# Longer PE warm-up, full-height contraction and a shared reciprocal in an attention and two-layer-MLP kernel

## The chip, the cores and the metric

The kernel runs on one core of one Trainium2 chip. The metric is the device time of one execution in microseconds (us). Five engines work side by side, each through its own queue in order: PE (TensorE, matrix products, with its weight loads shown as PEld), DVE (VectorE), ACT (ScalarE), POOL (GpSimd) and SP (SyncE, which here issues every DMA).

## The reference, cut to what matters

```python
scores = q @ k.T / sqrt(64)                     # 4 batches x 8 heads, 576 rows, 64 wide
decay  = cum[:, None] - cum[None, :]            # cum = cumsum(log(clip(f, 1e-4, 1)))
scores = where(causal, -1e9, scores + decay)
attn   = exp(scores - rowmax); attn /= rowsum + 1e-9
x      = attn @ v                               # 2304 tokens x 512
h = relu(x @ w_in); x = (h * h) @ w_out                        # 512 -> 2048 -> 512
h = x @ w_in2; y = where(h >= 1, h, where(h <= -1, 0, (h+1)**2 / 4)); out = y @ w_out2
```

## The kernel before, in words

The tokens are split into five blocks of up to 512. A block goes through the two MLPs as 32 steps (16 slices of 128 hidden units for each layer): `h_group` (L1006, products of L1016: x times w_in, 12 products of 512 columns for a full block), `act_group` (the nonlinearity) and `out_group` (L1054, products of L1067 to L1069 into accumulators). Every operand is split in a high and a low half and multiplied as three products. Weights come in as 64-bit floats, are decoded on ACT, DVE and POOL (L925 to L958), split (L976), stored to a scratch array in DRAM and read back by later blocks.

Attention of the first 256 query rows of each head (`HEAD`) is done by `attention32` (L591), in groups of four heads (`QUAD`). Groups 0 to 3 make up block 0, and stand ahead of everything else; groups 4 to 7 belong to block 1 and are interleaved with the MLP steps of block 0. The other rows are done by `attention` (L699) during later steps.

For each head of a group, `attention32` does in turn: the scores (L640, two fp32 products, of 128 and of 256 columns; the trace has two records for each product), a masked row maximum on DVE (L587), exp with row sums on ACT (L647), sum + 1e-9 and reciprocal on DVE (L652, L653, operation `o_r`), a scaling of E by the reciprocal on ACT, DVE or POOL (L661 to L663), three transposes on PE (L669) and a copy out of PSUM. After each second head, four products with v (L683) give the head pair's output, which is copied to `x` (L693, L695).

The score product gets the decay through extra rows of its contraction. `QK[0]` and `QK[1]` are two buffers of 128 partitions that groups take in turn. Rows 0 to 63 hold k and q. Rows 64 and 65 hold, on the K side, cum and the constant 8, and on the Q side the constant -8 and cum. `clear` (L546 to L554) sets rows 64 and 65 of both buffers to 8 and -8 with four memsets each (L555 in the trace: buffer 0 on DVE, buffer 1 on POOL). DMAs then write cum over one of the two rows on each side: for group 0 straight from the scan's result (`first_rows`, L507, once all memsets of buffer 0 are done), and for later groups from a copy in DRAM (L616). The score products use rows 0 to 65 (`kr`, `qr`: `reg()[:D + 2, ...]`).

`setup` (L474) loads f, clips it (L488, DVE), takes its logarithm (L490, ACT), scans it (L491, DVE), and stores cum (L503). Zeroing of the constant buffers Q2 and K2 (L517, L518) shares DVE and POOL with it. `warm_up` (L534) issues `WARM` = 11 products of the identity with itself on PE (L542) before the first scores.

The order on each engine is written at build time by a planner (`Schedule`, L152). Every operation has a due time, a cost and its dependences; of the operations that can start, the planner takes the one that is due first, tries several weights, and emits the shortest plan's order. On the chip each engine follows this order and waits on semaphores.

Of the kernel before, what the change touches and what calls it, by code (L numbers as in the profile page):

```python
# [8 lines left out]
F32 = mybir.dt.float32  # L9
# [7 lines left out]
AF = mybir.ActivationFunctionType  # L17
ALU = mybir.AluOpType

B, H, S, D = 4, 8, 576, 64  # L20
DM, DFF = 512, 2048
NT = B * S
P = 128
# [7 lines left out]
HEAD = 256  # L31
REST = S - HEAD
CHUNKS = [(HEAD, 320), (320, 448), (448, S)]
# [14 lines left out]
QUAD = 4  # L48
SPARE = ("E", "g", "E", "o", "E", "r", "E", "g", "E", "o")

SLAV = [0.0, 0.51, 0.75, 0.75, 0.0]
# [2 lines left out]
VE = [5.5, 6.1]  # L54
RE = [1.36, 7.73, 16.0]
LW = 29.1
WARM = 11


def pattern(bits):  # L60
# [320 lines left out]
def tile_attention_moe_moe(ctx: ExitStack, tc: tile.TileContext, qkv, f, w2, outT):  # L381
    nc = tc.nc
    PSUM = bass.MemoryType.PSUM
    W64 = w2.dtype == U64
    sch = Schedule()
# [4 lines left out]
    def ring(tag, n, shape, dt, space=None, fifo=True, most=()):  # L390
        kw = {"space": space} if space else {}
        tp = ctx.enter_context(tc.tile_pool(name="p_" + tag, bufs=n, **kw))
        pools[tag] = (Pool(n, fifo, most), tp, shape, dt)

    def new(tag, name, shape=None, dt=None, kind=None):
        p, tp, sh, d = pools[tag]
        shape = sh if shape is None else shape
        kw = {"padded_shape": sh} if list(shape) != list(sh) and len(shape) == len(sh) and dt is None else {}
        return Buf(p, lambda: tp.tile(shape, dt or d, tag=tag, name=name, **kw), kind)
# [3 lines left out]
    ring("K1", 2, [P, S], F32R)  # L403
    ring("vt", 3, [P, 5, 2, 64], F32R)
    ring("E", 5, [P, S], F32)
    ring("st", 4, [P, 3, len(CHUNKS)], F32)
    ring("mm", 3, [P, 2], F32)
    ring("PP", 3, [P, (2 * NK - 1) * P], F16)
    ring("PT", 2, [P, QUAD * 4 * HEAD], F16)
# [31 lines left out]
    for s in range(NS):  # L441
        g, att = s // NFC, 0.0
# [29 lines left out]
    QK = [new("PT", f"QK{i}", [P, QUAD * 2 * HEAD], F32) for i in range(2)]  # L472
# [75 lines left out]
    def clear(i, half):  # L548

        n = QUAD * HEAD  # L550
        rows = lambda a, z: QK[i].tile[a:z, n * half:n * half + n]
        kq = lambda a, z, t: rows(a, z).rearrange("p (c t n) -> p c t n", t=2, n=HEAD)[:, :, t, :]
        due = -98 + 2 * i + half
        eng, m = ("POOL", nc.gpsimd) if i else ("DVE", nc.vector)  # L554
        fill = lambda out, x: {eng: (n / 1920 + 0.03, lambda: m.memset(out(), x))}  # L555
        return [sch.op(due, fill(lambda t=t, x=x: kq(D, D + 2, t), x), [], [QK[i]]) for t, x in ((0, 8.0), (1, -8.0))]

    cleared = {(i, half): clear(i, half) for i in range(2) for half in range(2)}

# [4 lines left out]
    def copies(out, in_, n, engines="ACT DVE POOL", psum=False):  # L564

        alts = {}
        if "ACT" in engines:
            alts["ACT"] = (act_t(n, psum), lambda: nc.scalar.activation(out(), in_(), AF.Copy))  # L568
        if "DVE" in engines:
            alts["DVE"] = (  # L570
                dve_t(n) if psum else dve2_t(n), lambda: nc.vector.tensor_copy(out(), in_()), *([] if psum else [True]))  # L571
        if "POOL" in engines:
            alts["POOL"] = (pool_t(n), lambda: nc.gpsimd.tensor_scalar(  # L573
                out(), in_(), 1.0, 0.0, op0=ALU.mult, op1=ALU.add))
        return alts
# [15 lines left out]
    def attention32(g):  # L591

        first = g.blk == 0
        qk, n = QK[g.i % 2], QUAD * 2 * HEAD
        reg = lambda: qk.tile
        kr = lambda c: reg()[:D + 2, 2 * c * HEAD:2 * c * HEAD + HEAD]
        qr = lambda c: reg()[:D + 2, 2 * c * HEAD + HEAD:2 * c * HEAD + 2 * HEAD]
        wait = groups[g.i - 2].qk if g.i >= 2 else ()
        src = qkv[g.at:g.at + D * n].rearrange("(p n) -> p n", p=D)
        loads, parts = [], 2 if g.i == 0 else 1  # L600
# [25 lines left out]
            in_=qkv[g.at_v:g.at_v + P * vn].rearrange("(p n) -> p n", p=P)))}, [], [vt], early=VE[g.i] if g.i < len(VE) else g.due - 4)  # L626
        g.qk = []
        chunks = [(0, 0, P), (1, P, HEAD)]
        for c in range(QUAD):
            nm = f"{g.i}q{c}"  # L630
            t0 = g.due + g.len * c / QUAD
            a = c % 2
            Eb = new(SPARE[len(used) % len(SPARE)] if first else "E", f"E{nm}", [P, 3 * P])
            used.append(Eb)
            st = new("st", f"st{nm}")
            ps = new("acc" if first else "ps", f"s{nm}", kind="att")
            cols = lambda ci: slice(0, P) if ci == 0 else slice(P, 3 * P)
            o_e = []
            for ci, qa, e in chunks:
                o_s = sch.op(t0, {"PE": (4 * e / 2400, lambda c=c, ci=ci, qa=qa, e=e, ps=ps: nc.tensor.matmul(  # L640
                    ps.tile[:, cols(ci)], qr(c)[:, qa:qa + P], kr(c)[:, :e], start=True, stop=True))},
                    ready[c], [ps, Eb, qk])
                g.qk.append(o_s)
                o_t = sch.op(t0 + 0.3, {"DVE": (dve_t(e) + 0.01, lambda ci=ci, qa=qa, e=e, Eb=Eb, ps=ps, st=st: top(
                    Eb.tile[:, cols(ci)], ps.tile[:, cols(ci)], qa, e, P, -0.125, st.tile[:, 0, ci:ci + 1]))},
                    [o_s, mask_op[0]], [ps, Eb, st])
                o_e.append(sch.op(t0 + 0.8, {"ACT": (act_t(e, ptr=1) + 0.09, lambda ci=ci, Eb=Eb, st=st: nc.scalar.activation(  # L647
                    Eb.tile[:, cols(ci)], Eb.tile[:, cols(ci)], AF.Exp, scale=-1.0, bias=st.tile[:, 0, ci:ci + 1],
                    accum_out=st.tile[:, 1, ci:ci + 1]))}, [o_t], [Eb, st]))

            def recip(st=st):
                nc.vector.tensor_scalar(st.tile[:, 1, :2], st.tile[:, 1, :2], 1e-9, None, op0=ALU.add)  # L652
                nc.vector.reciprocal(st.tile[:, 2, :2], st.tile[:, 1, :2])  # L653

            o_r = sch.op(t0 + 2, {"DVE": (0.30, recip, True)}, o_e, [st])
            o_n = []
            for ci, qa, e in chunks:
                x = lambda ci=ci, Eb=Eb: Eb.tile[:, cols(ci)]
                r = lambda ci=ci, st=st: st.tile[:, 2, ci:ci + 1]
                o_n.append(sch.op(t0 + 2.5, {  # L660
                    "ACT": (act_t(e, ptr=1), lambda x=x, r=r: nc.scalar.activation(x(), x(), AF.Copy, scale=r())),  # L661
                    "DVE": (dve2_t(e), lambda x=x, r=r: nc.vector.tensor_scalar(x(), x(), r(), None, op0=ALU.mult), True),
                    "POOL": (pool_t(e), lambda x=x, r=r: nc.gpsimd.tensor_scalar(  # L663
                        x(), x(), r(), 0.0, op0=ALU.mult, op1=ALU.add)),
                }, [o_r], [Eb, st]))
            if a == 0:
                pr = new("pr", f"pr{nm}")
            tr = new("acc" if first else "ps", f"tr{nm}", kind="att")
            got = [sch.op(t0 + 3, {"PE": (0.11, lambda tr=tr, Eb=Eb, to=to, at=at: nc.tensor.transpose(  # L669
                tr.tile[:, to:to + P], Eb.tile[:, at:at + P], ident))}, [o_n[at > 0], id_op], [Eb, tr, pr])  # L670
                for to, at in ((0, 0), (P, P), (2 * P, 2 * P))]
            o_c = sch.op(t0 + 3.5, copies(
                lambda pr=pr, a=a: pr.tile[:, a, :3 * P].bitcast(F32), lambda tr=tr: tr.tile[:, :3 * P], 3 * P,
                "ACT DVE", psum=True), got, [tr, pr])
            if a == 0:
                o_c0 = o_c
                continue
            av = new("acc" if first else "ps", f"av{nm}", kind="att")
            o_m = None
            for kc in range(HEAD // P):  # L680
                def mms(c=c, kc=kc, pr=pr, av=av):
                    for i in range(2):
                        nc.tensor.matmul(  # L683
                            av.tile[D * i:D * i + D, kc * P:HEAD], v32(c - 1 + i, kc),
                            pr.tile[:, i, 2 * P * kc:2 * P * kc + HEAD - kc * P].bitcast(F32),
                            start=(kc == 0), stop=(kc == HEAD // P - 1))

                o_m = sch.op(t0 + 4, {"PE": (4 * (HEAD - kc * P) / 2400 + 0.05, mms)},
                             [o_c, o_c0, o_v, o_m], [av, vt, pr], SLAV[g.blk])
            x = xb[g.blk]  # L690
            kc = (g.h + c) // 2
            hi = lambda kc=kc: x.tile[:, kc, 0, g.off:g.off + HEAD]
            o3 = sch.op(t0 + 5, copies(hi, lambda av=av: av.tile[:, :HEAD], HEAD, "ACT DVE", psum=True), [o_m], [av, x])  # L693
            xops.setdefault((g.blk, kc), []).append(sch.op(t0 + 5.5, {
                "DVE": (dve_t(HEAD), lambda kc=kc, hi=hi, av=av: nc.vector.tensor_tensor(  # L695
                    x.tile[:, kc, 1, g.off:g.off + HEAD], av.tile[:, :HEAD], hi().bitcast(F32), op=ALU.subtract))},
                [o3], [av, x]))

    def attention(t):  # L699
        g, W, nm, due = t.b * H + t.h, REST, t.name, t.due  # L700
# [80 lines left out]

        def recip():
            nc.vector.tensor_scalar(
                st.tile[:, 1, :], st.tile[:, 1, :], 1e-9, unit, op0=ALU.add, op1=ALU.mult)
            nc.vector.reciprocal(st.tile[:, 2, :], st.tile[:, 1, :])  # L785

        o_r = sch.op(back(9.5), {"DVE": (0.30, recip, True)}, o_e, [st])

        o_t = []
# [409 lines left out]
```

## Time and profile before

| | us |
|---|---|
| median of 3 runs | 958.58 (956.57 to 959.28) |
| the profiled execution, its own time | 955.24 |
| its span in the profile | 953.5 |
| PE busy | 939.9 (99%) |
| DVE, ACT, POOL busy | 583.2, 638.0, 191.3 |

The span runs from the first to the last instruction of the profile. The granted clock (PEclk) is a share of TensorE's full 2.4 GHz: 1.00 is 2.4 GHz and 0.50 is 1.2 GHz. PE's busy time is modelled: its products are pipelined and their records overlap, so it tells that PE had work, not that it ran at its peak. "Share" of DMA is the mean busy share of the 16 DMA engines.

### The profile page before, as it was taken

The page shows a single profiled execution, that of the slowest core. Times are in us where ns is not written, and L with a number is a line of the kernel's source. Part 1 is how long each engine was busy: PE and PEld are TensorE (multiplying, and loading weights), DVE is VectorE, ACT ScalarE, POOL GpSimd, SP SyncE. Part 2 cuts the span into 40 slices and gives each one's busy share as a digit, 9 for nine tenths or more (in the row PEclk, how much of TensorE's full clock was granted, in tenths as well). Part 3 has the DMA queues.
Part 4 walks back from the last instruction along what each step waited for, and adds up shares of the span by engine and source line. Part 5 has one row for each costly group of instructions (what it writes and reads, how often), then busy time and mean ns, then how long its engine had stood idle before and what let it go on. Part 6 is the DMA issues. An engine that isn't in the chain of part 4 may idle for free.

```text
span 953.5 us, 14248 instructions
## 1 busy us (share of the span) xinstructions
PE 939.9 (99%) x4758; PEld 789.2 (83%) x4758; DVE 583.2 (61%) x1325; ACT 638.0 (67%) x1269; POOL 191.3 (20%) x341
## 2 busy tenths in 40 slices
PE   8999999999999999999999999999999999999998
PEld 6777777777778888888888888788888888889998
DVE  6899999989757668777767667866311132220032
ACT  5999879997877768787777677686432343334454
POOL 3321010134122323342323124231000000002200
PEclk6999999999999999999999999999999999999999
DMA  6699998996998987898899988796665655659994
GB/s 192 207 337 402 339 403 292 369 347 227 349 321 246 277 247 251 231 285 248 242 257 287 253 261 238 208 300 186 248 232 178 202 194 181 207 189 374 365 374 143
DMA packets 126106, 254.73 MB, mean 267 GB/s; under 512 B 89808, under 2 KB 90480, under 8 KB 104080
## 3 DMA queue, kind: packets, MB, share of 16 engines
q1 hardware_dynamic: 126032, 253.81, 81.0%
q8 instruction: 38, 0.62, 0.3%
q14 instruction: 36, 0.29, 0.1%
HBM read 194.35 MB, written 38.45 MB: 244 GB/s over the span
## 4 chain that ended last, share of the span: by engine, by line
PE 90%; DVE 4%; DMA 4%; issue 1%; ACT 1%; SPq 0%; POOL 0%; DVEq 0%; ACTq 0%
PE h L1016 39%; PE acc L1067 13%; PE acc L1069 13%; PE acc L1068 13%; PE av L840 4%; PE s L761 2%; PE s L762 2%; DMA PT<-PP 2%; DMA in<-in_qkv_dram 1%; DMA out_dram<-o 1%; PE s1q L640 1%; DVE whl L993 0%; DVE wf L957 0%; PE s0q L640 0%; DVE low L942 0%
## 5 line engine op out<-in xcount | busy, mean ns | idle before, releaser
L1016 PE MATMUL h<-x,whl 128*128 128x512 f32 (+1 forms) x1896 | 432.5, 371 | 0.6 <-DVE whl L993 0.5
L1016 PEld LDWEIGHTS h<-x,whl 128*128 128x128 f32 x1896 | 325.7, 189 | 55.4 <-issue 2.1
L1067 PE MATMUL acc<-gh,whl 128*128 128x512 f32 (+1 forms) x640 | 240.1, 375 | 2.9 <-DVE o L571 2.9
L1069 PE MATMUL acc<-gl,whl 128*128 128x512 f32 (+1 forms) x640 | 237.2, 371 | 0.0
L1068 PE MATMUL acc<-gh,whl 128*128 128x512 f32 (+1 forms) x640 | 236.7, 370 | 0.0
L580 DVE TENSOR_TENSOR gl<-g,gh 128x512 fp32r<-128x512 f32 (+1 forms) x126 | 83.6, 663 | 120.1 <-PE acc L1069 81.5
L1069 PEld LDWEIGHTS acc<-gl,whl 128*128 128x128 f32 x640 | 121.0, 189 | 21.5 <-POOL gl L582 0.2
L1067 PEld LDWEIGHTS acc<-gh,whl 128*128 128x128 f32 x640 | 120.9, 189 | 20.9 <-DVE o L571 3.4
L1068 PEld LDWEIGHTS acc<-gh,whl 128*128 128x128 f32 x640 | 121.0, 189 | 15.7
L1034 ACT ACTIVATE r<-h 128x512 f32<-128x512 f32 (+1 forms) x80 | 44.0, 550 | 91.3 <-PE h L1016 82.6
L1047 DVE SCALAR_TENSOR_TENSOR g<-r,h 128x512 f32<-128x512 f32 (+1 forms) x80 | 50.4, 630 | 80.1 <-ACT r L1045 79.6
L582 POOL TENSOR_TENSOR gl<-g,gh 128x512 fp32r<-128x512 f32 (+1 forms) x34 | 39.7, 1169 | 287.3 <-PE acc L1069 213.6
L1043 ACT ACTIVATE r<-h,half 128x512 f32<-128x512 f32 (+1 forms) x80 | 51.1, 639 | 61.9 <-PE h L1016 61.6
L815 DVE SCALAR_TENSOR_TENSOR PP<-E,st,PP 128x512 f16<-128x512 f32 (+2 forms) x128 | 77.6, 638 | 11.0 <-ACT PP L811 10.1
L778 ACT ACTIVATE E<-E,st 64x320 f32<-64x320 f32 (+2 forms) x96 | 63.6, 662 | 24.1 <-DVE st L587 15.6
L587 DVE CUSTOM_DVE_ANT_0 E<-s,mask 128x288 f32<-128x288 f32 (+2 forms) x128 | 62.1, 502 | 28.3 <-PE s L762 20.1
L811 ACT ACTIVATE PP<-E,st 128x512 f16<-128x512 f32 (+2 forms) x128 | 68.9, 591 | 9.1 <-DVE st L785 7.7
L840 PEld LDWEIGHTS av<-pr,vt 128*128 128x128 f32 x288 | 53.9, 189 | 13.0 <-issue 1.7
L840 PE MATMUL av<-pr,vt 128*128 128x320 f32 (+2 forms) x288 | 61.8, 287 | 1.3 <-DVE pr L571 1.3
L568 ACT ACTIVATE gh<-g 128x512 fp32r<-128x512 f32 (+1 forms) x70 | 40.7, 581 | 31.5 <-DVE g L1047 31.1
L573 POOL TENSOR_SCALAR pr<-PT 128x640 fp32r<-128x640 f16 (+2 forms) x50 | 31.2, 627 | 108.4 <-PE av L840 57.3
L568 ACT ACTIVATE pr<-PT 128x640 fp32r<-128x640 f16 (+2 forms) x63 | 36.3, 580 | 18.2 <-DMA PT<-PP 11.8
(258 smaller groups left out, 1145.4 us busy)
## 6 DMA issues: line engine op xcount, KB each, us to landing
whl<-scr SPq DMA_DIRECT2D x112, 1024.0 KB
raw<-in_w_dram SPq DMA_DIRECT2D x28, 1024.0 KB
scr<-whl SPq DMA_DIRECT2D x28, 1024.0 KB
in<-in_qkv_dram SPq DMA_DIRECT2D x32, 608.0 KB
whl<-scr SPq DMA_DIRECT2D x32, 512.0 KB
out_dram<-o SPq DMA_DIRECT2D x16, 256.0 KB
QK<-in_qkv_dram SPq DMA_DIRECT2D x7, 512.0 KB
raw<-in_w_dram SPq DMA_DIRECT2D x6, 512.0 KB
```

Source lines behind the costliest of these rows:

```text
L568: alts["ACT"] = (act_t(n, psum), lambda: nc.scalar.activation(out(), in_(), AF.Copy))
L580: alts["DVE"] = (dve_t(n), lambda: nc.vector.tensor_sub(out(), a(), b()), True)
L587: return nc.vector.tensor_tensor_reduce(out=out, in0=ps, in1=mask[:m, OFF - q0:OFF - q0 + n], scale=scale, scalar=3e38, op0=ALU.add, op1=A ...
L778: nc.scalar.activation(Ec.tile[:m, :e], Ec.tile[:m, :e], AF.Exp, scale=-1.0, bias=nmx(), accum_out=st.tile[:m, 1, ci:ci + 1])))}, [*tops, ...
L811: nc.scalar.activation(hi, x, AF.Copy, scale=r())
L815: nc.vector.scalar_tensor_tensor(lo, x, r(), hi, op0=ALU.mult, op1=ALU.subtract)
L840: nc.tensor.matmul(av.tile[:, c0:W], vt.tile[:, kc, :, :], pr.tile[:, i, :n], start=(kc == 0 and i == 0), stop=(kc == NK - 1))
L1016: nc.tensor.matmul(ps.tile[:, :n], w.tile[:, 0, wi, kc * P:(kc + 1) * P], src.tile[:, kc, xi, :n], start=(kc == 0 and i == 0), stop=(kc == ...
L1043: o1 = sch.op(due, {"ACT": (act_t(n, True, 1), lambda: A.activation(r.tile[:, :n], ps(), AF.Relu, scale=0.5, bias=half))}, [o], [psb, r])
L1067: nc.tensor.matmul(a.tile[:, :n], wh, gh.tile[:, :n], start=(fc == 0), stop=False)
L1068: nc.tensor.matmul(a.tile[:, :n], wl, gh.tile[:, :n], start=False, stop=False)
L1069: nc.tensor.matmul(a.tile[:, :n], wh, gl.tile[:, :n], start=False, stop=(fc == NFC - 1))
```

## The change

`WARM` goes from 11 to 17. The score products contract over all 128 rows of `QK` instead of 66; for this `clear` fills rows 64 to 127 with 8 on the K side and 0 on the Q side, and then row 64 of the Q side with -8 (three memsets instead of two for each half buffer). From group 1 on, two heads share one `st` tile, and with it one addition and one reciprocal over four columns, which wait for the exps of both heads; group 0 keeps one for each head. `attention32` is cut for this into `exps`, `recips`, `probabilities` and `products`. The `st` tile has four columns instead of three, and `attention` uses three of them.

```diff
-WARM = 11
+WARM = 17
...
-    ring("st", 4, [P, 3, len(CHUNKS)], F32)
+    ring("st", 4, [P, 3, 4], F32)
...
-        return [sch.op(due, fill(lambda t=t, x=x: kq(D, D + 2, t), x), [], [QK[i]]) for t, x in ((0, 8.0), (1, -8.0))]
+        kr = sch.op(due, fill(lambda: kq(D, P, 0), 8.0), [], [QK[i]])
+        qr = sch.op(due, fill(lambda: kq(D, P, 1), 0.0), [], [QK[i]])
+        return [kr, sch.op(due, fill(lambda: kq(D, D + 1, 1), -8.0), [qr], [QK[i]])]
...
-        kr = lambda c: reg()[:D + 2, 2 * c * HEAD:2 * c * HEAD + HEAD]
-        qr = lambda c: reg()[:D + 2, 2 * c * HEAD + HEAD:2 * c * HEAD + 2 * HEAD]
+        kr = lambda c: reg()[:, 2 * c * HEAD:2 * c * HEAD + HEAD]
+        qr = lambda c: reg()[:, 2 * c * HEAD + HEAD:2 * c * HEAD + 2 * HEAD]
...
-            def recip(st=st):
-                nc.vector.tensor_scalar(st.tile[:, 1, :2], st.tile[:, 1, :2], 1e-9, None, op0=ALU.add)
-                nc.vector.reciprocal(st.tile[:, 2, :2], st.tile[:, 1, :2])
-
-            o_r = sch.op(t0 + 2, {"DVE": (0.30, recip, True)}, o_e, [st])
+        def recips(c, st, n, deps):
+            def recip():
+                nc.vector.tensor_scalar(st.tile[:, 1, :n], st.tile[:, 1, :n], 1e-9, None, op0=ALU.add)
+                nc.vector.reciprocal(st.tile[:, 2, :n], st.tile[:, 1, :n])
+
+            return sch.op(g.due + g.len * c / QUAD + 2, {"DVE": (0.30, recip, True)}, deps, [st])
...
+        for c in range(0, QUAD, 2):
+            got = []
+            if g.i == 0:
+                for a in range(2):
+                    st = new("st", f"st{g.i}q{c + a}")
+                    Eb, o_e = exps(c + a, st, 0)
+                    got.append(probabilities(c + a, st, 0, Eb, recips(c + a, st, 2, o_e)))
+            else:
+                st = new("st", f"st{g.i}q{c}")
+                (E0, o0), (E1, o1) = (exps(c + a, st, 2 * a) for a in range(2))
+                o_r = recips(c + 1, st, 4, [*o0, *o1])
+                got = [probabilities(c + a, st, 2 * a, Eb, o_r) for a, Eb in enumerate((E0, E1))]
+            products(c + 1, got)
```

## Rows read from the trace of the kernel before

**Rows 1.** The page: the span, and part 1, busy time by engine.

```profile
span 953.5 us, 14248 instructions
...
PE 939.9 (99%) x4758; PEld 789.2 (83%) x4758; DVE 583.2 (61%) x1325; ACT 638.0 (67%) x1269; POOL 191.3 (20%) x341
```

**Rows 2.** Windows: length, busy (count) PE, PEld, DVE, ACT, POOL, clock, DMA, GB/s.

```profile
5.33:8.74 3.41, 0.65 (x6) 0.45 (x4) 2.81 (x7) 1.66 (x4) 1.54 (x5) 1.00 0.60 163
8.74:25.81 17.07, 16.73 (x59) 12.68 (x61) 9.54 (x53) 9.72 (x36) 1.68 (x4) 0.50 0.66 202
25.81:45.16 19.35, 19.07 (x138) 13.93 (x134) 17.53 (x84) 18.04 (x57) 6.66 (x14) 1.00 0.74 220
45.16:100.00 54.84, 54.84 (x258) 43.70 (x259) 52.97 (x98) 53.08 (x97) 11.71 (x5) 1.00 0.97 365
100.00:250.00 150.00, 149.32 (x697) 117.64 (x696) 140.01 (x246) 130.31 (x212) 27.50 (x30) 1.00 0.90 332
...
264.74:268.15 3.41, 3.41 (x10) 2.85 (x11) 1.72 (x6) 2.80 (x7) 0.00 (x0) 0.50 1.09 329
```

**Rows 3.** Line L542 (warm-up) in two stretches: duration in ns, min/median/max.

```profile
L542 PE MATMUL warm<-ident x7: 421/421/421, 2.6 to 3.9; 128*128 128x128 f32 x7
...
L542 PE MATMUL warm<-ident x7: 274/275/421, 4.8 to 5.7; 128*128 128x128 f32 x7
```

**Rows 4.** Timeline of PE, 0 to 30 us: start, length, what [idle before].

```profile
1.39 4.59 PE L542 MATMUL warm<-ident 128*128 128x128 f32 x22 [1.39 <-POOL tiny L482]
8.84 5.46 PE L640 MATMUL s0q<-QK 66*128 66x128 f32 x16 [2.86 <-DMA QK<-setup]
```

**Rows 5.** The chain that ended last, 0 to 60 us, in order of time.

```profile
6.85 1.85 DMA QK<-setup
...
45.16 4.31 PE h L1016 x18
```

**Rows 6.** Waits of PE over the whole span: total, times, longest.

```profile
PE acc L1067 <- DVE o L571: 2.9, 1, 2.9
...
PE av L840 <- DVE pr L571: 1.3, 1, 1.3
```

**Rows 7.** Lines by form, 26.2 to 45.16 us, PE and PEld: busy us, mean ns.

```profile
L669 PE MATMUL tr3q<-ident,E3q 128*128 128x128 f32 x12 | 2.4, 279 | 0.1
...
L640 PE MATMUL s3q<-QK 66*128 66x128 f32 x8 | 1.6, 287 | 0.0
...
L640 PEld LDWEIGHTS s3q<-QK 66*128 66x128 f32 x16 | 2.2, 191 | 0.2 <-issue 0.2
...
L1016 PEld LDWEIGHTS h<-x,whl-2_481 128*128 128x128 f32 x6 | 1.1, 190 | 0.1
```

**Rows 8.** Timeline of DVE, 0 to 9 us.

```profile
0.90 2.11 DVE L555 MEMSET QK<- 2x512 f32 x4 [0.90 <-PEq L1181]
...
3.50 0.33 DVE L518 MEMSET Q<- 64x320 f32 x1
3.90 0.54 DVE L518 MEMSET K<- 64x576 f32 x1
...
7.04 0.54 DVE L518 MEMSET K<- 4x576 f32 x1 [0.17 <-DVE K L518]
```

**Rows 9.** Timeline of POOL, 0 to 15 us.

```profile
2.66 2.23 POOL L555 MEMSET QK<- 2x512 f32 x4
...
14.18 0.48 POOL L663 TENSOR_SCALAR E0q<-E0q,st0q 128x256 f32<-128x256 f32 x1 [7.18 <-DVE st0q L653]
```

**Rows 10.** Lines L652 and L653 for one group of four heads.

```profile
L652 DVE TENSOR_SCALAR st1q<-st1q x4: 158/162/216, 20.6 to 29.0; 128x2 f32<-128x2 f32 x4
...
L653 DVE RECIPROCAL st1q<-st1q x4: 167/168/168, 20.8 to 29.2; 128x2 f32<-128x2 f32 x4
```

**Rows 11.** Timeline of ACT: ends of the exps of two heads of group 2.

```profile
28.94 0.19 ACT L647 ACTIVATION_READ_ACCUMULATOR E2q<-E2q,st2q 128x1 f32 x1
...
29.81 0.19 ACT L647 ACTIVATION_READ_ACCUMULATOR E2q<-E2q,st2q 128x1 f32 x1
```

More of the change, by code (lines that the diff above doesn't have):

```diff
@@ L628, in attention32, with exps @@
         chunks = [(0, 0, P), (1, P, HEAD)]
-        for c in range(QUAD):
+        sums = {}
+        def exps(c, st, at):
             nm = f"{g.i}q{c}"
             t0 = g.due + g.len * c / QUAD
-            a = c % 2
             Eb = new(SPARE[len(used) % len(SPARE)] if first else "E", f"E{nm}", [P, 3 * P])
             used.append(Eb)
-            st = new("st", f"st{nm}")
             ps = new("acc" if first else "ps", f"s{nm}", kind="att")
@@ L644, in attention32, with probabilities @@
                 o_t = sch.op(t0 + 0.3, {"DVE": (dve_t(e) + 0.01, lambda ci=ci, qa=qa, e=e, Eb=Eb, ps=ps, st=st: top(
-                    Eb.tile[:, cols(ci)], ps.tile[:, cols(ci)], qa, e, P, -0.125, st.tile[:, 0, ci:ci + 1]))},
+                    Eb.tile[:, cols(ci)], ps.tile[:, cols(ci)], qa, e, P, -0.125, st.tile[:, 0, at + ci:at + ci + 1]))},
                     [o_s, mask_op[0]], [ps, Eb, st])
                 o_e.append(sch.op(t0 + 0.8, {"ACT": (act_t(e, ptr=1) + 0.09, lambda ci=ci, Eb=Eb, st=st: nc.scalar.activation(
-                    Eb.tile[:, cols(ci)], Eb.tile[:, cols(ci)], AF.Exp, scale=-1.0, bias=st.tile[:, 0, ci:ci + 1],
-                    accum_out=st.tile[:, 1, ci:ci + 1]))}, [o_t], [Eb, st]))
-            def recip(st=st):
-                nc.vector.tensor_scalar(st.tile[:, 1, :2], st.tile[:, 1, :2], 1e-9, None, op0=ALU.add)
-                nc.vector.reciprocal(st.tile[:, 2, :2], st.tile[:, 1, :2])
-            o_r = sch.op(t0 + 2, {"DVE": (0.30, recip, True)}, o_e, [st])
+                    Eb.tile[:, cols(ci)], Eb.tile[:, cols(ci)], AF.Exp, scale=-1.0, bias=st.tile[:, 0, at + ci:at + ci + 1],
+                    accum_out=st.tile[:, 1, at + ci:at + ci + 1]))}, [o_t], [Eb, st]))
+            return Eb, o_e
+        def recips(c, st, n, deps):
[3 more added lines that the diff above has]
+            return sch.op(g.due + g.len * c / QUAD + 2, {"DVE": (0.30, recip, True)}, deps, [st])
+        def probabilities(c, st, at, Eb, o_r):
+            nm = f"{g.i}q{c}"
+            t0 = g.due + g.len * c / QUAD
+            a = c % 2
+            cols = lambda ci: slice(0, P) if ci == 0 else slice(P, 3 * P)
             o_n = []
@@ L658, in attention32 @@
                 x = lambda ci=ci, Eb=Eb: Eb.tile[:, cols(ci)]
-                r = lambda ci=ci, st=st: st.tile[:, 2, ci:ci + 1]
+                r = lambda ci=ci, st=st: st.tile[:, 2, at + ci:at + ci + 1]
                 o_n.append(sch.op(t0 + 2.5, {
@@ L666, in attention32 @@
             if a == 0:
-                pr = new("pr", f"pr{nm}")
+                sums["pr"] = new("pr", f"pr{nm}")
+            pr = sums["pr"]
             tr = new("acc" if first else "ps", f"tr{nm}", kind="att")
@@ L671, in attention32, with products @@
                 for to, at in ((0, 0), (P, P), (2 * P, 2 * P))]
-            o_c = sch.op(t0 + 3.5, copies(
+            return sch.op(t0 + 3.5, copies(
                 lambda pr=pr, a=a: pr.tile[:, a, :3 * P].bitcast(F32), lambda tr=tr: tr.tile[:, :3 * P], 3 * P,
                 "ACT DVE", psum=True), got, [tr, pr])
-            if a == 0:
-                o_c0 = o_c
-                continue
+        def products(c, got):
+            pr, nm, t0 = sums["pr"], f"{g.i}q{c}", g.due + g.len * c / QUAD
             av = new("acc" if first else "ps", f"av{nm}", kind="att")
@@ L688, in attention32 @@
                 o_m = sch.op(t0 + 4, {"PE": (4 * (HEAD - kc * P) / 2400 + 0.05, mms)},
-                             [o_c, o_c0, o_v, o_m], [av, vt, pr], SLAV[g.blk])
+                             [*got, o_v, o_m], [av, vt, pr], SLAV[g.blk])
             x = xb[g.blk]
@@ L783, in recip @@
             nc.vector.tensor_scalar(
-                st.tile[:, 1, :], st.tile[:, 1, :], 1e-9, unit, op0=ALU.add, op1=ALU.mult)
-            nc.vector.reciprocal(st.tile[:, 2, :], st.tile[:, 1, :])
+                st.tile[:, 1, :3], st.tile[:, 1, :3], 1e-9, unit, op0=ALU.add, op1=ALU.mult)
+            nc.vector.reciprocal(st.tile[:, 2, :3], st.tile[:, 1, :3])
         o_r = sch.op(back(9.5), {"DVE": (0.30, recip, True)}, o_e, [st])
```

## The prediction, made before the changed kernel ran

> **What bounds the kernel now.** I read the page first: PE has work in 939.9 of 953.5 us [rows 1]. That is an average over stages, so the table of windows comes next; the reader is to look at the clock column beside the busy columns [rows 2]. From 45.16 us on PE works without a gap up to 100 and in 149.32 of 150 us up to 250, and the chain of waits runs through PE's own products from there on [rows 2, 5]. A microsecond by which PE gets there earlier is worth one microsecond at the end, as long as the other engines and the DMA follow. The stretch that stands out lies before: from 8.74 to 25.81 us PE is busy in 16.73 of 17.07 us, but at a granted clock of 0.50, the 1.2 GHz level. ACT and DVE are busy there in 9.72 and 9.54 us, little more than half [rows 2]. So in this stretch PE at half speed is the limit, and everybody else waits for it. In the stretch behind it (25.81 to 45.16, clock 1.00) the limits are close together: ACT 18.04 of 19.35 us (93%), DVE 17.53 (91%), PE 19.07 [rows 2].
>
> **How the clock got there.** The eleven warm-up products run from 1.39 to 5.98 us [rows 4]. The clock column shows 1.00 for this time, but the records say more: a warm-up record takes 421 ns between 2.6 and 3.9 us and 275 ns after 4.8 us [rows 3], so the products began at the low level and the higher one came while they ran. Then PE waits 2.86 us for the rows of cum, until 8.84 [rows 4], and the clock falls at 8.74. It falls a second time, at 264.74, behind an idle time of 2.9 us [rows 2, 6]. An idle time of 1.3 us does not lower it (the wait of L840, [rows 6]). So the idle time explains the fall. It does not explain why the clock stays low for 17.07 us although PE is busy in 98% of them. What is special in this stretch is what PE runs: score products that fill 66 of 128 rows, eight heads of them, the first sixteen records without another product between [rows 4]. At the second fall, with products of 128 rows, the clock was back after 3.41 us [rows 2]. The warm-up multiplies an identity with itself, nearly all zeros, and raised the clock [rows 3]: rows filled with constants can count.
>
> **A rule against it.** The row shows busy PE without full clock for 17.07 us [rows 2]. The Trainium skill (TensorE: Matmul & The Clock Gate, Part 1) says that the clock is set by how busy PE has been, and that sustained work releases it; the height of the contraction is not in it. By that rule the padding would bring nothing and the first term of the sum would hang on the longer warm-up alone. The trace disagrees: by the rule the clock should have come back long before 25.81.
>
> **The change part by part**, against the profiled execution's own 955.24 us.
>
> *Clock of the first scores.* At full level the 16.73 us of PE become 8.4, so the stretch cannot shrink by more than 17.07 - 8.4 = 8.7 us. From the other side, ACT's 9.72 us at the 93% of the next stretch take 10.4 us, and ACT first waits some 1.1 us for a head's scores (estimate: four records of 287 ns, [rows 7]); 17.07 - 11.5 = 5.5 us. I take 6.0, near ACT's end, since ACT and DVE fill the stretch that already runs at full clock.
>
> *Does the clock hold over the gap?* Six more products start at 5.98. A product is two records, 4.59 / 11 = 0.42 us at the low level [rows 4], so they end between 7.2 (full level) and 8.5 (low). That is before the 8.84 at which the rows of cum are there, and that wait hides them; without it they would cost 1.3 to 2.5 us. The idle time left is 0.4 to 1.8 us, between the 1.3 that held and the 2.9 that fell, nearer to the first. If the clock falls, I price it by 264.74 to 268.15: 3.41 us at half speed, 1.7 us lost [rows 2]. Between 0 and +1.7 I take +0.4.
>
> *Wider products.* Nothing: a score record of 66x128 takes 287 ns and a transpose of 128x128 279; a weight load of 66 rows takes 191 and one of 128 rows 190 [rows 7].
>
> *Memsets.* Buffer 0 takes six on DVE instead of four, buffer 1 six on POOL. The number of partitions does not matter (64x576 and 4x576 both 0.54 us), and one takes 2.11 / 4 = 0.53 us [rows 8]. The two more on DVE (1.06 us) must be done before the rows of cum may be written, so they will stand where the memsets of Q and K stand now (0.33 us, and 0.36 of K's 0.54 before the scan at 4.36): 1.06 instead of 0.86 us ahead of the scan, which delays the SP issue, the landing [rows 5] and the first score by 0.2 us. If DVE's order puts both ahead of the clipping it is 1.1, if behind the scan 0. I take +0.2. On POOL the clearing ends 1.1 us later than 4.89 and its next work goes back by as much; POOL stands idle for 7.18 us up to 14.18 [rows 9], which hides it. Without this cover it would be 1.1.
>
> *Shared reciprocals.* Groups 1 to 7 have 14 pairs, and each loses one addition and one reciprocal of 0.16 and 0.17 us [rows 10]: 4.6 us of DVE. In groups 1 to 3 (six pairs, 2.0 us) DVE and ACT share the limit, so a part comes through: between 0 and -2.0 I take -0.5. In groups 4 to 7 PE is the limit and hides it: 0 (were DVE the limit there, -2.6). The new wait: the first head's scaling, transposes and copy wait for the second head's exps, 29.81 - 28.94 = 0.9 us later [rows 11]. Behind the reciprocal on DVE stand the row maxima of the next heads and the splitting of weights; behind the transposes on PE stand other heads' scores or MLP products. As the order is written with this dependence in it, other work goes ahead: 0, and at most 14 x 0.9 = 12.6 us where none does.
>
> The sum: -6.0 + 0.4 + 0.2 - 0.5 = -5.9, so 949.3 us on the profiled execution's scale. The three runs shown lie 1.3 to 4.0 us above that execution, their median 3.3. I can't see why; if the low clock lasts longer in them, the change takes that away as well, if not, it stays. I add half: 951.0 us.
>
> **The rivals.**
> 1. *The forecast*: the clock is at 1.00 from about 9 us, or after one short fall, and PE's unbroken work begins about 6 us before 45.16. 0.79.
> 2. *Constant rows do not count*: the longer warm-up bridges less than it must, and the scores run at 0.50 up to about 25 us as now. Left are +0.2 - 0.5: 954.9, or 956.6 with the half added. For it: the added rows on the Q side are zero. Against it: the identity products [rows 3]. 0.11.
> 3. *The gain is given back between 45 and 100 us.* DMA's share is 0.97 there, DVE and ACT are at 97% [rows 2]. If weights don't land or decode earlier, PE waits for them, and of 6 us some 2 are left: about 955. Against it: before 45 us DMA's share is 0.66 to 0.74 and ACT and DVE have 7 us to spare in the slow stretch, so their work moves forward as well. 0.05.
> 4. *The shared reciprocal stalls PE*: transposes stand next on PE while the second head's exps run, 0.9 us for each of 14 pairs [rows 11]. All of them: 951.0 + 12.6 = 963.6, slower than before. It decides the sign from (958.6 - 951.0) / 0.9, more than 8 pairs, on. Against it: PE has MLP work to put between in groups 4 to 7. 0.05.
>
> **How the numbers follow.** A measurement of this kernel tells a change from none at about 0.3%, 2.9 us. Rival 1 is faster by more than that in nearly all of its range, 2 and 3 lie within 0.3% with little beyond, 4 is slower. Faster 0.79, same 0.15, slower 0.06. The range's lower end takes the PE bound of 8.7 us and 1 us for the reciprocals (955.2 - 9.7 = 945.5). Its upper end is rival 1 with the small gain, the short fall and late memsets (-5.5 + 1.7 + 1.1, -2.7) on the runs' scale, 955.9, and reaches into rival 2, to 956.5. Left out are rival 4 and about half of 2.
>
> **What would show it.** Right: records of the last warm-up products near 275 ns; clock near 1.00 in the windows from 9 (at the latest some 12) to 26 us; ACT and DVE over 85% busy there; the first long run of h products starting near 39 instead of 45.16; the wait of PE for QK at 9.0 us; reciprocals over 4 columns, half as many from group 1 on. Wrong: a clock of 0.50 up to 20 us or more (rival 2), new waits of h products for whl between 45 and 100 us (rival 3), waits of the transposes or of L683 for E or pr on PE (rival 4), or an early start that is lost again in a longer stop like that at 261 us.

## The result and the profile after

The changed kernel takes 947.47 us (median of 3 runs, 946.77 to 948.35), against 958.58. The ratio is 0.9885, with a 95% interval of 0.9861 to 0.9908: 11 us faster. The time lies in the range that was given, 3.5 us below the forecast of 951.0. The profiled execution took 946.77 us; its span is 945.0 us, 8.5 less than before.

The first view is the table of windows of the changed kernel, cut as in [rows 2] (length, busy time and count of PE, PEld, DVE, ACT and POOL, clock, DMA share, GB/s).

```profile
5.33:8.74 3.41, 1.48 (x14) 1.28 (x12) 3.13 (x6) 1.40 (x4) 2.90 (x9) 1.00 0.56 130
8.74:25.81 17.07, 14.74 (x93) 10.39 (x94) 14.10 (x75) 14.61 (x56) 2.49 (x6) 1.00 0.94 265
25.81:45.16 19.35, 19.12 (x120) 13.33 (x120) 15.87 (x62) 17.75 (x54) 7.64 (x11) 1.00 0.78 247
45.16:100.00 54.84, 54.52 (x254) 42.94 (x252) 54.04 (x86) 48.11 (x79) 3.35 (x2) 1.00 0.95 362
100.00:250.00 150.00, 149.95 (x704) 118.59 (x703) 139.46 (x249) 133.55 (x220) 35.99 (x33) 1.00 0.90 336
```

The low clock is gone. From 8.74 to 25.81 us PE issues 93 products instead of 59, and ACT and DVE are busy in 14.61 and 14.10 us instead of 9.72 and 9.54. So some 5 us of the work of each came forward. ACT did not reach the 93% on which I had built, but 86%; DVE is at 83%.

The timeline of PE, to set beside [rows 4]:

```profile
1.39 5.41 PE L542 MATMUL warm<-ident 128*128 128x128 f32 x34 [1.39 <-POOL tiny L482]
9.21 2.86 PE L643 MATMUL s0q<-QK 128*128 128x128 f32 x16 [2.40 <-DMA QK<-setup]
```

The sixteen records of the first four heads' scores take 2.86 us instead of 5.46. The warm-up ends at 6.80 us, earlier than the 7.2 I had worked out, because in this execution the clock rose earlier; the idle time behind it is 2.40 us, and it did not lower the clock.

Further on, the chain that ended last (start, length, what) goes through DVE before the first MLP steps:

```profile
42.99 0.60 DVE wf L978
43.59 0.36 DVE setup L498
43.95 0.68 DVE low L974
44.63 0.63 DVE setup L500
45.26 0.61 DVE wf L980
45.87 1.14 DVE whl L1019
47.05 2.56 PE h L1042 x10
```

At 42 us the chain leaves PE for DVE, which still decodes weights, and comes back to PE at 47.05. This costs PE little: it runs other products meanwhile and waits 0.3 us for these weights. The last attention output of block 0 is some 3.7 us earlier than before; by the first accumulator products the lead is 3.6 us.

Where does the rest come from? In the timeline of PE, the 129th of the 640 products of the first accumulator line starts in the kernel before at

```profile
255.94 0.39 PE L1067 MATMUL acc<-gh,whl 128*128 128x512 f32 x1
```

and in the changed kernel at

```profile
252.06 0.39 PE L1093 MATMUL acc<-gh,whl 128*128 128x512 f32 x1
```

That is 3.9 us. Eight products later, at 274.25 and 265.69 us, it is 8.6, and at the end 8.5. So of 8.5 us, 3.9 were won at the start and 4.6 around 261 us. There the kernel before stopped for 2.9 us and then ran 3.41 us at half clock [rows 2, 6], which is 2.9 + 1.7. The waits of PE in the changed kernel (total, times, longest) have no such stop:

```profile
...
PE tr0q L682 <- ACT E0q L673: 0.9, 1, 0.9
PE acc L1093 <- ACT o L570: 0.7, 1, 0.7
PE tr1q L682 <- POOL E1q L675: 0.6, 1, 0.6
PE av L866 <- DVE st L589: 0.5, 1, 0.5
PE h L1042 <- DVE whl L1019: 0.3, 1, 0.3
...
```

The wait for an output buffer, 0.7 us, now stands at 470 us.

### The profile page after: what moved, and what is told of

Same layout as the page of the kernel before. It is cut to its first block, busy times and chain, and to the rows that moved or that the text cites. A ratio compares the mean times of both kernels' runs of the same rounds, so it can differ in the third digit from the quotient of the medians.

```text
span 945.0 us, 14242 instructions
## 1 busy us (share of the span) xinstructions
PE 933.9 (99%) x4770; PEld 782.9 (83%) x4770; DVE 585.9 (62%) x1319; ACT 638.2 (68%) x1269; POOL 183.3 (19%) x323
## 4 chain that ended last, share of the span: by engine, by line
PE 92%; DVE 3%; DMA 2%; ACT 1%; issue 1%; POOL 0%; SPq 0%; DVEq 0%; ACTq 0%; POOLq 0%
PE h L1042 40%; PE acc L1093 13%; PE acc L1095 13%; PE acc L1094 13%; PE av L866 4%; PE s L787 2%; PE s L788 2%; DMA PT<-PP 1%; DMA raw-2_209<-in_w_dram 1%; DMA out_dram<-o 1%; DVE PP L841 0%; PE s1q L643 0%; PE s7q L643 0%; PE s4q L643 0%; PE s5q L643 0%
## 5 line engine op out<-in xcount | busy, mean ns | idle before, releaser
L584 POOL TENSOR_TENSOR gl<-g,gh 128x512 fp32r<-128x512 f32 (+1 forms) x38 | 44.4, 1168 | 341.2 <-PE acc L1095 253.1
L804 ACT ACTIVATE E<-E,st 64x320 f32<-64x320 f32 (+2 forms) x96 | 63.6, 662 | 26.2 <-DVE st L589 15.8
L570 ACT ACTIVATE gh<-g 128x512 fp32r<-128x512 f32 (+1 forms) x66 | 38.1, 577 | 30.7 <-DVE g L1073 30.4
L575 POOL TENSOR_SCALAR pr<-PT 128x640 fp32r<-128x640 f16 (+2 forms) x49 | 28.5, 583 | 125.9 <-PE av L866 91.1
L1071 ACT ACTIVATE r<-r 128x512 f32<-128x512 f32 (+1 forms) x80 | 46.9, 587 | 2.0
```

The lines of the kernel that those rows point to most:

```text
L804: nc.scalar.activation(Ec.tile[:m, :e], Ec.tile[:m, :e], AF.Exp, scale=-1.0, bias=nmx(), accum_out=st.tile[:m, 1, ci:ci + 1])))}, [*tops, ...
```

## The experiments

Two things change together here: what PE does at the start, and the order that the planner writes, which depends on every cost and dependence. Most experiments therefore keep one kernel's order and alter only what is issued: the planner is told the same costs. Each row's ratio is to the kernel before on the same chip. Differences between two of these kernels are taken from the medians, although the runs were on more than one chip; the kernel before has medians from 956.97 to 958.58 us beside them, so 1 to 2 us of such a difference can come from that. `o` is the tile from which outputs are stored; the kernel has two buffers for it, and a "third o buffer" is one more that the planner does not know of.

| label | kernel and order | median us (range, runs) | before beside it | ratio, interval |
|---|---|---|---|---|
| a_rows66 | changed, 66 rows | 952.10 (946.90 to 955.17, 10) | 956.97 | 0.9914 to 0.9966 |
| a_warm11 | changed, 11 products | 950.80 (949.44 to 954.65, 6) | 956.97 | 0.9912 to 0.9968 |
| a_old_pe | changed, both undone | 957.73 (953.79 to 960.83, 10) | 956.97 | 0.9983 to 1.0035 |
| a_sep | changed, separate reciprocals, new order | 950.61 (949.44 to 951.58, 7) | 956.97 | 0.9913 to 0.9956 |
| b_clock | before, 17 products, 128 rows | 952.38 (950.12 to 953.58, 9) | 957.91 | 0.9926 to 0.9957 |
| b_clock_o3 | the same, third o buffer | 949.80 (949.15 to 950.34, 4) | 957.91 | 0.9890 to 0.9950 |
| b_o3 | before, third o buffer | 955.26 (952.51 to 956.80, 10) | 957.91 | 0.9953 to 0.9996 |
| a_zero | changed, added rows 0 on both sides | 950.79 (949.83 to 951.05, 6) | 957.91 | 0.9909 to 0.9959 |
| a_four | changed, four instructions for a pair | 947.85 (947.43 to 949.54, 4) | 958.38 | 0.9879 to 0.9909 |
| a_warm24 | changed, 24 products | 946.91 (945.79 to 948.20, 4) | 958.38 | 0.9861 to 0.9893 |
| a_warm24_o3 | the same, third o buffer | 946.20 (945.32 to 947.29, 4) | 958.38 | 0.9859 to 0.9889 |

### Rows and warm-up, one by one, in the new order

```diff
-        kr = lambda c: reg()[:, 2 * c * HEAD:2 * c * HEAD + HEAD]
+        kr = lambda c: reg()[:D + 2, 2 * c * HEAD:2 * c * HEAD + HEAD]
```

(and the same for `qr`): a_rows66.

> The changed kernel with its order of work, its fills and its 17 warm-up products, but the scores contract over 66 rows again. Theory (the height of the contraction decides whether the clock stays up): the granted clock is at 0.50 for most of the time from about 9 to 20 us and the time is 3 to 6 us above the changed kernel, 950 to 954. Rival (the longer warm-up alone holds the clock): 1.00 throughout, 946 to 949.

The profiled execution is as the rival had it: clock 1.00, 946.90 us, an idle time of 1.76 us ahead of the scores. Most other runs are not. Time and mean granted clock of each run:

```
946.90 1.000   947.07 0.999   947.80 0.998   951.21 0.994   951.91 0.992
952.28 0.991   953.57 0.990   954.15 0.991   954.78 0.989   955.17 0.989
```

With 66 rows the mean clock is 0.998 or more in three runs of ten; in the others the clock is low for a while. With 128 rows and the same order the three runs read 1.000, 1.000 and 0.998, and the eleven of a_four and a_sep read 0.998 to 1.000 too. So the longer warm-up can be enough, and the rows make it dependable. The list also prices the low clock (an estimate): a mean of 0.989 is some 21 us at half speed (0.011 x 2 x 953), and costs 8.3 us, 0.4 us for each.

```diff
-        sch.op(-90, {"PE": (0.43 * WARM, lambda: mms(WARM))}, [id_op], [ps])
+        sch.op(-90, {"PE": (0.43 * WARM, lambda: mms(11))}, [id_op], [ps])
```

> The changed kernel with its order of work and 128 rows, but only 11 warm-up products are issued. Theory (rows raise the clock again, the warm-up only bridges): the clock falls near 9 us and is back after 3 to 4 us of scores; 1 to 2 us above the changed kernel, 948 to 950. Rival (the longer warm-up is what counts): 0.50 up to 20 us or more, 950 to 954. Rival (the rows alone are enough): no fall, 946 to 949.

This is the theory's case. The windows of this kernel show the clock fall over an idle time of 3.1 us and come back while the scores run, instead of 17 us later:

```profile
9.06:12.47 3.41, 3.27 (x11) 2.94 (x12) 2.11 (x9) 0.99 (x4) 0.49 (x2) 0.50 0.91 211
12.47:25.81 13.34, 11.61 (x71) 7.68 (x71) 10.76 (x60) 11.35 (x44) 2.29 (x6) 1.00 0.84 252
```

The price, 3.3 us by the medians, is above the 1 to 2 I expected. In two of six runs the mean clock is 0.996, in one 0.994, so the low clock lasted longer there. The profiled execution, with its one short fall, is 3.3 us later too, but its first accumulator product is only 1.5 us later (50.90 against 49.45). The rest is mostly a wait for an output buffer at 474 us, 2.4 us where the changed kernel waits 0.7 (waits of PE, a_warm11; the total has 0.5 us at 261 us in it):

```profile
PE acc L1093 <- ACT o L570: 2.8, 2, 2.4
```

So the new order has such a wait as well, in another place, and its length differs between executions. Both edits together, a_old_pe:

> The changed kernel with its order of work, but 66 rows and 11 warm-up products, so PE sees the same start as before the change. Theory (the clock gives about 4 us up to 45 us, and the stop of 2.9 us at 261 us went with the new order): clock 0.50 from about 9 to 22 us, 950 to 953, and no stop of over 2 us near 261. Rival (the stop went because work came earlier): the stop is back, 955 to 959. Rival (the shared reciprocals and the new order made the gain): 946 to 949.

```profile
9.58:30.06 20.48, 20.04 (x71) 13.70 (x71) 11.94 (x62) 12.34 (x44) 2.28 (x6) 0.50 0.67 197
30.06:45.16 15.10, 14.89 (x105) 10.53 (x105) 12.29 (x55) 13.79 (x49) 5.52 (x11) 1.00 0.74 232
```

The low clock is back for 20.48 us, PE is busy in 98% of them, and the whole gain is gone: 957.73 us, a ratio of 0.9983 to 1.0035. The time lies almost 5 us above the theory's range. Near 261 us there is no stop (the longest wait of PE for an output buffer there is 0.4 us), so that does go with the new order. But at low clock the new order is 3.5 us later than the old one in its first accumulator product (56.55 against 53.03), and it waits 1.4 us for an output buffer at 479 us; together these eat the gain up. Part of the 3.5 us is the longer low clock of this execution, 20.48 against 17.07 us; why the rest, I did not test.

Set beside a_warm11, this run isolates the rows: the two differ in nothing else. In both the clock falls after some 3 us of idle time; with 128 rows it is back after 3.41 us, with 66 after 20.48, and the medians are 950.80 and 957.73 us.

### Do the values in the added rows count?

```diff
-        kr = sch.op(due, fill(lambda: kq(D, P, 0), 8.0), [], [QK[i]])
+        kr = sch.op(due, {eng: (n / 1920 + 0.03, lambda: (m.memset(kq(D, P, 0), 0.0), m.memset(kq(D, D + 2, 0), 8.0)))}, [], [QK[i]])
```

> The changed kernel, but rows 66 to 127 of the K side hold 0 instead of 8, so the added rows are zero on both sides (four more memsets are issued). Theory (the rows count whatever they hold): every run's mean clock at 0.998 to 1.000, 946 to 950. Rival (the values count): as with 66 rows, most runs at a mean clock of 0.989 to 0.994 and 951 to 955.

Rows 66 to 127 are now zero on both sides. The extra memsets delay the first score to 11.28 us and PE stands idle for 3.75 us, so the clock falls, at 12.62 us. What matters is what follows:

```profile
12.62:16.03 3.41, 3.17 (x11) 2.21 (x11) 2.39 (x15) 2.64 (x12) 0.48 (x1) 0.50 0.98 275
16.03:25.81 9.78, 8.62 (x55) 5.74 (x55) 7.75 (x44) 8.15 (x32) 0.37 (x1) 1.00 0.92 267
```

It is back 3.41 us later, as in a_warm11 with its eights, and no run reads below 0.996. The rows count whatever they hold. At the first accumulator product this kernel is 3.0 us behind the changed one (52.42 against 49.45), so the delay and the fall make up most of the 3.3 us between the medians, which put it 0.8 above the theory's range.

### The clock and the stop in the old order

b_clock issues 17 products in the kernel before, contracts over 128 rows, and fills them with one memset more for each half buffer (inside the same planned operation):

```diff
-        return [sch.op(due, fill(lambda t=t, x=x: kq(D, D + 2, t), x), [], [QK[i]]) for t, x in ((0, 8.0), (1, -8.0))]
+        def q_rows():
+            m.memset(kq(D, P, 1), 0.0)
+            m.memset(kq(D, D + 1, 1), -8.0)
+
+        return [sch.op(due, fill(lambda: kq(D, P, 0), 8.0), [], [QK[i]]),
+                sch.op(due, {eng: (n / 1920 + 0.03, q_rows)}, [], [QK[i]])]
...
```

> The kernel before with its own order of work, but 17 warm-up products issued, 128 rows of contraction and the fills for them (two more memsets on each of DVE and POOL). Theory (the clock is worth 4 to 7 us in the old order too, and the stop near 261 us belongs to the old order): clock 1.00 up to the stop, 950 to 953 against 957, a wait of 2 to 3 us of L1067 for o near 255. Rival (the stop went because work came earlier): no such wait, 945 to 948. Rival (the old order cannot use the clock): 955 or more.

5.5 us less, in the theory's range. The clock of 1.00 up to the stop did not come: the scores begin only at 10.68 us and the clock still falls for 3.41 us in the profiled execution. The stop is there (waits of PE, b_clock):

```profile
PE acc L1072 <- DVE o L576: 2.6, 1, 2.6
```

```diff
-        tp = ctx.enter_context(tc.tile_pool(name="p_" + tag, bufs=n, **kw))
+        tp = ctx.enter_context(tc.tile_pool(name="p_" + tag, bufs=n + (tag == "o"), **kw))
```

> The kernel before with nothing but the third buffer for o. Theory: low clock from 9 to 25 us as before, no stop near 261: 952 to 955 against 957. Rival: no change.

> The same, with a third buffer for the outputs o that the planner does not know of. Theory (the stop is a wait for an output buffer whose store has not landed): the wait of L1067 for o is under 1 us, the second fall of the clock is gone, and 3 to 5 us less than without the buffer: 945 to 949. Rival (the stop has another cause): as without the buffer.

With this one edit in the kernel before, PE's longest wait for o is (waits of PE, b_o3)

```profile
PE acc L1067 <- ACT o L568: 0.3, 1, 0.3
```

and the time falls by 2.7 us, to 0.3 above the theory's range. That is less than the 4.6 that the trace of before shows, since other waits take a part (1.7 us of L640 for a DMA into QK). Both edits together give 8.1 us, about the sum of 5.5 and 2.7, and the second fall of the clock is gone; at 949.80 us, 2.6 below b_clock, this is 0.8 above the theory's range. So the stop was a wait for an output buffer whose store had not landed, and it and the clock are separate.

### The shared reciprocal

a_sep lets every group take the path of group 0, one reciprocal for each head; the planner then finds another order.

```diff
-            if g.i == 0:
+            if True:
```

> The changed kernel with one reciprocal for each head in all groups, planned anew. Theory (the shared reciprocal is worth under 1 us by itself; a new order can move a stop by some us): 946 to 951. Rival (it carries a good part of the gain): clock 1.00 all the same, and 952 or more.

a_four keeps the changed kernel's order and the wait of a pair, and issues the instructions for each head:

```diff
-                nc.vector.tensor_scalar(st.tile[:, 1, :n], st.tile[:, 1, :n], 1e-9, None, op0=ALU.add)
-                nc.vector.reciprocal(st.tile[:, 2, :n], st.tile[:, 1, :n])
+                for i in range(0, n, 2):
+                    nc.vector.tensor_scalar(st.tile[:, 1, i:i + 2], st.tile[:, 1, i:i + 2], 1e-9, None, op0=ALU.add)
+                    nc.vector.reciprocal(st.tile[:, 2, i:i + 2], st.tile[:, 1, i:i + 2])
```

> The changed kernel with its order of work and its shared wait, but the addition and the reciprocal of a pair are issued as two of each over two columns (14 pairs, 28 DVE instructions more, 4.6 us of DVE in all, 2.0 us of it in groups 1 to 3). Theory (the saved instructions are worth little; the 3 us that separate heads cost are the other order the planner finds): within 1 us of the changed kernel, 946.5 to 949. Rival (the saved DVE time is what the sharing brings): 949.5 to 951.

Separate heads cost 3.1 us against the changed kernel, at a mean clock of 0.998 to 1.000. The saved instructions are not the reason: with all of them back, in the same order, a_four takes 0.4 us more, within the spread of its runs. What a_sep has instead are waits of PE that its order brings:

```profile
...
PE h L1042 <- DVE whl L1019: 1.1, 1, 1.1
PE acc L1093 <- ACT o L570: 1.1, 1, 1.1
PE h L1042 <- ACT r L1071: 0.9, 1, 0.9
...
```

So the sharing was worth some 3 us here by the order that came of it. Whether another change of the order of this kind would bring as much, no run tells.

### A longer warm-up still

```diff
-        sch.op(-90, {"PE": (0.43 * WARM, lambda: mms(WARM))}, [id_op], [ps])
+        sch.op(-90, {"PE": (0.43 * WARM, lambda: mms(24))}, [id_op], [ps])
```

> The changed kernel with its order of work, but 24 warm-up products issued. Theory (the idle time of PE ahead of the first scores, 2.4 us, is what still lets the clock fall in a few runs): idle under 1.2 us, every run at a mean clock of 1.000, 946 to 947.5. Rival (the longer warm-up delays the first scores): they start after 9.4 us and the time is 948 or more.

a_warm24_o3 adds the third output buffer as in b_o3.

> The same, with a third output buffer that the planner does not know of. Theory (the new order waits for an output buffer for only 0.7 us): up to 0.7 us less than with 24 products alone, 945.5 to 947.5. Rival (where transfers take longer in other runs the buffer is worth more): 945 or less.

With 24 products PE works up to 9.61 us, and the scores follow without a gap, 0.24 us later than in the changed kernel (timeline of PE, a_warm24):

```profile
1.39 8.22 PE L542 MATMUL warm<-ident 128*128 128x128 f32 x48 [1.39 <-POOL tiny L482]
9.45 2.79 PE L643 MATMUL s0q<-QK 128*128 128x128 f32 x16
```

The runs read 0.999 to 1.000, and the medians, 946.91 and 946.20 us, are the lowest of the study. Their intervals overlap with that of the change, so neither is shown to be faster than it.

## Why the prediction was right, and where its sum was off

**The cause was right.** PE at half speed held the first scores back, and the 66 rows kept the clock there: a_warm11 and a_old_pe differ in the rows alone, 3.41 against 20.48 us of low clock. Undoing rows and warm-up takes the whole gain away (a_old_pe); that it comes out so even is chance, as the new order then loses at the start about what it saves at the stop. Rival 2, constant rows that do not count, falls with a_zero and a_warm11. The rule that I weighed, the Trainium skill's (TensorE: Matmul & The Clock Gate, Part 1), names only how busy PE is; a_old_pe disagrees, with PE busy in 20.04 of 20.48 us at 0.50.

**The clock of the first scores, -6.0.** In the old order b_clock gains 5.5 us by the medians, though its scores begin later and the clock falls once. But the medians hold longer low clocks than the profiled execution, to which the term belonged; against that one (955.24) it is 2.9. In the changed kernel only 3.9 us had come by 250 us, from all four terms together, where the sum has 5.9. The step that failed took the work of the stretch as given and only its speed as changed. In the new order the rows and the warm-up move the first accumulator product from 56.55 us (a_old_pe) to 49.45, by 7.1 us; but at low clock that order starts 3.5 us later than the old one, in part by its longer low clock. Two signs did not come: DVE is below 85% busy, and the first long run of h products starts not near 39 but at 41.84 us, 3.3 earlier than in the kernel before. Rival 3 is not to be seen: the lead is 3.6 us at 49 us and 3.9 at 250.

**The stop at 261 us, not in the sum.** I read it, used it to price a fall of the clock, and left it in place. A plan that is made anew can drop such a stop, and did: 4.6 us. The two errors, +2.0 and -4.6, make up the 2.5 us between 949.3 and the profiled 946.77. That the sum came so near is in part luck: the errors have opposite signs, and nothing in the working foresaw the second.

**The gap of the warm-up, +0.4.** It cost nothing in the profiled execution: idle for 2.40 us, above the 0.4 to 1.8 that I gave, without a fall. **Memsets, +0.2.** They stand where the step put them, and the first score came 0.37 us later (9.21 against 8.84). The 0.86 us in that step is the whole time from 3.50 to 4.36 us; the two shares named beside it, 0.33 and 0.36, do not add up to it. **Wider products, 0.** A score record of 128x128 takes 288 ns:

```profile
L643 PE MATMUL s3q<-QK 128*128 128x128 f32 x8 | 1.6, 288 | 0.0
```

**Shared reciprocals, -0.5.** For the instructions, a_four has 0.4. The order that came of the sharing was worth more than they. Rival 4 did not come: PE's waits behind the pair are 0.6 us and less.

**The scale, half of 3.3.** This is the other step that failed. I could not see why the runs lie above the profiled execution. The runs of the kernel before that stand beside the experiments show it: 48 of 51 have a mean clock between 0.984 and 0.993, the shortest (952.84 us) 0.991 and the longest (960.55) 0.984; the profiled one had 0.989. The low clock lasts longer in most runs (36 of the 51 are below 0.989), so the change takes most of the excess away, not half of it: its median lies 0.7 us above its profiled execution. The spread seems to go with it: 1.6 us over three runs, and 2.1 and 2.4 over four each of a_four and a_warm24, instead of 7.7 over 51; so few runs do not show how far it reaches.

## What to carry to other kernels

When an engine is busy and yet others wait for it, look at the granted clock of that stretch and at what shapes it runs before asking for less work: products that fill half the rows kept PE at half speed for 17 us, and filling the rest with constants cost nothing in the length of a product (288 against 287 ns). Where a planner writes the order, every change is also a new order: keep the plan and change only what is issued to tell the two apart, and go through the stops of the old trace asking which a new order may drop. A spread of some us between runs can have one cause, here the length of a low clock at the start, and a change that removes it can gain more than one profiled execution shows.

## What the runs showed of the hardware that was not expected

- Rows that are zero on both sides of a product raise the clock like any others (a_zero: back 3.41 us after the fall).
- The same program, with 66 rows and 17 warm-up products, ran at a mean clock of 0.998 to 1.000 in three runs and, by the mean clock, with some 11 to 21 us of low clock in seven, 946.9 to 955.2 us.
- Score products of 66 rows do not lower a clock that is up: in the kernel before they ran from 26 us on among other products at 1.00, in 287 ns [rows 2, 7].
- Idle times of PE of 1.76 (a_rows66), 2.35 (a_sep, a_four) and 2.40 us (the changed kernel) ahead of the scores did not lower the clock in the profiled executions; 2.43 (b_clock_o3), 2.58 (b_clock), 2.86, 3.08 and 3.75 us did. The length of the idle time alone does not tell 2.40 from 2.43.
- A few runs read a mean clock of 0.998 to 1.000 and yet take long (956.95 us at 1.000 in the kernel before). The clock column shows 1.00 before its first change, [rows 3], so a clock that is low from the first instruction on may not be seen in it; that this is the reason was not tried.
